# Feed-forward seven slots behind its attention up to batch 4, and a shorter list of loads behind each w1

## The chip, the cores and the metric

The kernel runs on one core of one Trainium2 chip. The time is device microseconds of that core for one execution. An execution is called fast here when it is not in the chip's slower state. A profile is one execution taken by the hardware profiler; its span (from the first instruction to the last) is 1.6 to 2.0 us shorter than the time of the same execution. In the views PE is TensorE, DVE is VectorE, ACT is ScalarE, POOL is GpSimd and SP is SyncE. L251 is the line of the `kx` and `qx` copies, L267 that of all transposes, L504 the gate's maximum and L511 the first of w1's three requests.

## The reference

Eight batches go through masked attention, and then each through a feed-forward of one expert, which a gate picks from the mean of the attention's output. Cut to what matters:

```python
# q, k, v: (8 batches, 8 heads, 576, 64) float32
scores = q @ k.T / 8           # heads 0-3: 0 <= rel < 32; heads 4-7: rel < 128 and rel % 4 == 0
x = softmax(masked scores) @ v # -> (8, 576, 512)

pooled = x.mean(axis=1)        # one expert for a whole batch
e = argmax(pooled @ w_gate)    # 8 experts
h = maximum(x @ w1[e], 0.0)    # w1[e]: 512 x 1024
out = gate_w * (h @ w2[e])     # w2[e]: 1024 x 512
```

For this argument it matters that w1 and w2 of a batch (2.1 MB each in float32) can't be requested before that batch's attention is done and its gate has been decided, and that every batch brings new q, k, v and new weights.

## The kernel before

All work is laid out by hand in **slots**. A batch's attention takes four slots (4b to 4b+3), the first two with heads 4 to 7 ("g = 1"), the others with heads 0 to 3 ("g = 0"). Its feed-forward is cut into 21 **pieces**: 16 of the first matrix product, four output blocks of the second, and a tail. `PIECES` says how many pieces each slot gets beside its attention; the count runs on from batch to batch.

```python
NSLOT = 4
PIECES = [0] * 7 + [6, 6, 5, 2, 2] + [8, 8, 2, 3] * 7   # slots 0 to 39
GO = (1, 0)                                             # order of the halves
```

So batch 0's feed-forward is spread over slots 7 to 11, and that of batch b from 1 on fills slots 4b+8 to 4b+11, eight slots after its attention began. The slots loop, with cuts:

```python
for t in range(7, len(PIECES)):
    cur, pre = sl[t], sl[t - 1]
    ...
    gb, gn = divmod(t - 5, NSLOT)
    if gn == 0 and 0 < gb < B:
        emit_gate(gb)                  # first thing in slot 4b+5
    ...
    run_T(t)                           # transposes of the k or q of slot t+2 or t+1
    pre.av_a(); ...; cur.s(); cur.x()  # attention
    ...
    for f in items[:k0]: f()           # feed-forward pieces
    pre.norm()                         # the last one of a batch also makes `pooled`
    for b, g, nm in tsched.get(t + 1, []):
        if g == 0:
            emit_pair(b, nm)           # VectorE copies kx, qx for the next slot's transposes
    for f in items[k0:]: f()
```

The gate, with the loads that it requests behind its w1. All these loads are issued by GpSimd, in this order, and land in this order:

```python
def emit_gate(b):
    ...
    nc.tensor.matmul(lg, lhsT=pooled..., rhs=wg_t...)    # 4 matmuls
    nc.vector.max_with_indices(mx[:], mi[:], lg)
    e_val = nc.values_load(mi..., engines=[ET.Pool], ...)  # GpSimd waits for the index
    nc.gpsimd.dma_start(out=w1b[:, 2:4, :], in_=moe_w1[ds(e_val, 1), 256:512, :]...)
    ...                                                   # and the other half of w1
    if b == 0:
        load_va(2); load_qb(2); load_w2(e_val, w2b); load_qa(3); load_vb(2)
    else:
        load_vb(b + 2)
        load_w2(e_val, w2b)
        load_qa(b + 3)     # k and q of heads 4-7
    load_va(b + 3)
    load_qb(b + 3)         # k and q of heads 0-3

def emit_pair(b, nm):      # heads 0-3 only
    x = ldp.tile([P, RH, 2, DH], BF16, name=f"{nm}x", ...)
    nc.vector.tensor_copy(out=x..., in_=loads[b][nm, 0][:])
```

The q, k and v requested behind the gate of batch b are those of batch b+3, a whole batch ahead of need (all but `load_vb`, which is for batch b+2). Outputs are stored by SyncE, one slot after they are made (1.18 MB per batch).

The softmax here doesn't subtract the row's maximum and nothing guards it: scores larger than these inputs give would overflow.

Of the kernel before, what the change touches and what calls it, by code (L numbers as in the profile page):

```python
# [20 lines left out]
B = 8  # L21
# [21 lines left out]
HALF = 288  # L43
NSLOT = 4
EARLY = 7

PIECES = [0] * 7 + [6, 6, 5, 2, 2] + [8, 8, 2, 3] * 7


@with_exitstack  # L50
def kernel(
# [42 lines left out]
    def bank():  # L94
        return psM.tile([P, 512], F32, name="m", tag="M", space=PSUM)[:]
# [12 lines left out]
    def load_tiles(b):  # L108
        t = {}
        for g in range(2):  # L110
            for nm in ("k", "q"):
                shape = [P, RJ, DH] if g else [P, 2, RH, DH]
                t[nm, g] = ldp.tile(shape, BF16, name=f"{nm}m{g}", tag=f"{nm}m{g}")
            t["v", g] = ldp.tile([P, 4, 4, DH], BF16, name=f"vm{g}", tag=f"vm{g}")
        t["vt", 0] = ldp.tile([KB, 4, DH], BF16, name="vt0", tag="vt0")
        t["vt", 1] = ldp.tile([KB, 4, 2, DH], BF16, name="vt1", tag="vt1")
        loads[b] = t

    def load_1(b, g, nm):
        i = src[nm][b, 4 * g : 4 * g + 4]  # L120
        if g == 0:
            i = bass.AP(tensor=i.tensor, offset=i.offset, ap=[[RH * DH, P], [2 * S * DH, 2], [1, RH * DH]])
            nc.gpsimd.dma_start(out=loads[b][nm, g][:].rearrange("p h j d -> p h (j d)"), in_=i)
        else:
            i = i.rearrange("h s d -> (h s) d").rearrange("(p j) d -> p j d", j=RJ)
            nc.gpsimd.dma_start(out=loads[b][nm, g][:], in_=i)

    def load_qk(b, g):
        for nm in ("k", "q"):
            load_1(b, g, nm)  # L130

    def load_v(b, g):
        t = loads[b]["v", g]
        if g == 0:
            for h in range(4):
                nc.gpsimd.dma_start(out=t[:, h], in_=v[b, h, 0:512, :].rearrange("(c p) d -> p c d", p=P))  # L136
        else:
            nc.gpsimd.dma_start(out=t[:], in_=v[b, 4:8, 0:512, :].rearrange("h (p j) d -> p h j d", j=4))

    def load_vt(b, g):  # L140

        vt = loads[b]["vt", g]
        if g == 0:
            nc.gpsimd.dma_start(out=vt[:], in_=v[b, 0:4, 512:S, :].rearrange("h p d -> p h d"))
        else:
            nc.gpsimd.dma_start(out=vt[:], in_=v[b, 4:8, 448:S, :].rearrange("h (p t) d -> p h t d", t=2))

    GO = (1, 0)

    def load_qa(b):  # L150
        if b < B:
            load_tiles(b)
            load_qk(b, GO[0])

    def load_va(b):
        if b < B:
            load_v(b, GO[0])
            load_vt(b, GO[0])

    def load_qb(b):  # L160
        if b < B:
            load_qk(b, GO[1])

    def load_vb(b):
        if b < B:
            load_v(b, GO[1])
            load_vt(b, GO[1])
# [75 lines left out]
    def half(a):  # L243
        return slice(64 * a, 64 * a + 64)
# [250 lines left out]
    def emit_gate(b):  # L495
        s = st[b]
        pooled = s["pooled"]
        lg = bank()[0:1, 0:E]
        for c in range(4):
            nc.tensor.matmul(lg, lhsT=pooled[:, c : c + 1], rhs=wg_t[:, c, :], start=(c == 0), stop=(c == 3))  # L500
        l_sb = small.tile([1, E], F32, name="l_sb", tag="l_sb")
        mx = small.tile([1, 8], F32, name="mx", tag="mx")
        mi = small.tile([1, 8], U32, name="mi", tag="mi")
        nc.vector.max_with_indices(mx[:], mi[:], lg)  # L504
        nc.vector.tensor_copy(out=l_sb[:], in_=lg)
        s["gate"] = (l_sb, mx)
        e_val = nc.values_load(mi[0:1, 0:1].bitcast(I32), engines=[ET.Pool], min_val=0, max_val=E - 1)
        w2b = wp.tile([P, 8, DM], BF16, name="w2b", tag="w2b")
        w1b = wp.tile([P, 4, F], BF16, name="w1b", tag="w1b")
        s["w1"], s["w2"] = w1b, w2b  # L510
        nc.gpsimd.dma_start(  # L511
            out=w1b[:, 2:4, :],
            in_=moe_w1[ds(e_val, 1), 256:512, :].rearrange("e (c p) f -> p (e c) f", p=P),
        )
        for a in range(2):
            nc.gpsimd.dma_start(
                out=w1b[half(a), 0:2, :],
                in_=moe_w1[ds(e_val, 1), 128 * a : 128 * a + 128, :].rearrange("e (h d) f -> d (e h) f", d=DH),
            )
        if b == 0:  # L520
            load_va(2)
            load_qb(2)
            load_w2(e_val, w2b)
            load_qa(3)
            load_vb(2)
        else:
            load_vb(b + 2)
            load_w2(e_val, w2b)
            load_qa(b + 3)
        load_va(b + 3)  # L530
        load_qb(b + 3)

    def load_w2(e_val, w2b):

        nc.gpsimd.dma_start(
            out=w2b[:].rearrange("p (x j) f -> p x (j f)", x=2),
            in_=moe_w2[ds(e_val, 1)].rearrange("e (x p j) f -> p (e x) (j f)", x=2, p=P),
        )
# [16 lines left out]
    def emit_gate_bc(b):  # L555

        gw = st[b]["gw"]
        gbc = small.tile([P, 1], F32, name="gbc", tag="gbc")
        nc.sync.dma_start(out=gbc[:], in_=gw[0:1, 0:1].to_broadcast([1, P]))
        st[b]["gbc"] = gbc  # L560


    def ffn1(b, fc, hf, eng, cs=(2, 3, 0, 1)):
        s = st[b]
        if fc == 0 and hf == 0 and "ht" not in s:
            s["ht"] = htp.tile([P, 8, S], BF16, name="ht", tag="ht")
        cols = slice(HALF * hf, HALF * hf + HALF)
        if 2 in cs:
            s["hm"] = bank()[:, 0:HALF]
        hm = s["hm"]  # L570
        for c in cs:
            w = s["w1"][:, c, F // 2 * (fc // 4) : F // 2 * (fc // 4) + F // 2].rearrange("p (m j) -> p j m", j=4)
            nc.tensor.matmul(hm, lhsT=w[:, fc % 4, :], rhs=s["xt"][:, c, cols], start=(c == 2), stop=(c == 1))  # L573
        if 1 not in cs:
            return
        o = s["ht"][:, fc, cols]
        if eng == "A":
            nc.scalar.activation(out=o, in_=hm, func=AF.Relu)  # L578
        else:
            nc.vector.tensor_scalar_max(out=o, in0=hm, scalar1=0.0)  # L580
# [3 lines left out]
    def flush():  # L584
        for f in stores:
            f()
        stores.clear()
# [40 lines left out]
    for b in range(B):  # L628
        for n in (0, 2):
            t = NSLOT * b + n  # L630
# [3 lines left out]
    def run_T(t):  # L634
        for b, g, nm in tsched.get(t, []):
            for f in emit_T(b, g, nm):
                f()
# [41 lines left out]

    sl = [slot(t) for t in range(len(PIECES))]  # L680

# [10 lines left out]
    nd_banks = {"0dk": (0, 1), "0pk": (0, 1), "1dk": (2, 1), "1dq": (0, 2)}  # L692
    evac = {}

    def piece(b, x, e):
        if x < 16:
            ffn1(b, x // 2, x % 2, e)
        elif x < 20:
            ffn2(b, x - 16, "AD"[x % 2])
        else:  # L700
            ffn_tail(b)
# [35 lines left out]
    done = 0  # L737
    for t in range(7, len(PIECES)):
        cur, pre = sl[t], sl[t - 1]
        n = PIECES[t]  # L740

        lead = t > 7 and n >= 5 and done % 21 < 16 and pre.on
        items = []
        for i, x in enumerate(range(done, done + n)):
            e = "A" if ((lead or t == 7) and i == 0) or 2 * i >= n else "D"
            items.append(lambda x=x, e=e: piece(x // 21, x % 21, e))
        done += n
        gb, gn = divmod(t - 5, NSLOT)
        if gn == 0 and 0 < gb < B:
            emit_gate(gb)  # L750
        if t == 7:
            items.pop(0)
            n -= 1
            dve, act = emit_T(2, GO[0], "q")
            dve()
            act()
        else:
            run_T(t)
            pre.av_a()
            flush()  # L760
            if (t == 8) if gb == 0 else gn == 2 and gb < B:
                emit_gate_bc(gb)
            cur.s()
            cur.x()
            if pre.on and not cur.on:
                items.pop(0)()
                n -= 1
            pre.av_b()
            if lead:
                items.pop(0)()  # L770
                n -= 1
            pre.ln()
            cur.mask()
            pre.rd()
        k0 = n // 2
        for f in items[:k0]:
            f()
        if t > 7:
            pre.norm()
        for b, g, nm in tsched.get(t + 1, []):  # L780
            if g == 0:
                emit_pair(b, nm)
        for f in items[k0:]:
            f()
        if (t == 7) if gb == 0 else gn == 1 and gb < B:
            emit_gate_w(gb)
# [31 lines left out]
```

## Time and profile before

| | before |
|---|---|
| time, median of the 3 runs that the prediction had (lowest to highest) | 211.54 us (211.29 to 211.74) |
| span of the profiled run | 210.9 us |
| PE busy | 192.6 us, 91% |
| loads' packets, share of 16 engines' span | 96.2% |
| distance of gates from 43 to 158 us (first matmul of a gate to that of the next) | 22.3 to 23.5 us |

PE's row is not to be read alone: PE and DMA are both nearly full until all of q, k and v are in. The prediction below shows those rows, and the waits that tell which of the two is ahead. One view: the busy time of each engine in the stretch from 57 to 150 us, which is the steady state (columns: stretch, its length; busy us and instructions of PE, PE's weight loads, VectorE, ScalarE, GpSimd; granted clock; mean share of DMA packets in flight; GB/s). Before:

```profile
57.00:150.00 93.00, 88.60 (x1444) 65.89 (x1452) 62.74 (x172) 66.79 (x136) 40.50 (x60) 1.00 1.25 222
```

PE works 88.6 of 93 us, at full clock. Beside this row stands a number of mine, worked out from the same DMA records: for each 0.1 us, how many packets of loads and stores were in flight, on 16 engines. What is missing to 16, as a share of 16 and summed up from 57 to 150 us, is called **DMA idle** below. It is 0.04 us before.

### The profile page before, as it was taken

The page shows a single profiled execution, that of the slowest core. Times are in us where ns is not written, and L with a number is a line of the kernel's source. Part 1 is how long each engine was busy: PE and PEld are TensorE (multiplying, and loading weights), DVE is VectorE, ACT ScalarE, POOL GpSimd, SP SyncE. Part 2 cuts the span into 40 slices and gives each one's busy share as a digit, 9 for nine tenths or more (in the row PEclk, how much of TensorE's full clock was granted, in tenths as well). Part 3 has the DMA queues.
Part 4 walks back from the last instruction along what each step waited for, and adds up shares of the span by engine and source line. Part 5 has one row for each costly group of instructions (what it writes and reads, how often), then busy time and mean ns, then how long its engine had stood idle before and what let it go on. Part 6 is the DMA issues. An engine that isn't in the chain of part 4 may idle for free.

```text
span 210.9 us, 6979 instructions
## 1 busy us (share of the span) xinstructions
PE 192.6 (91%) x2906; PEld 140.1 (66%) x2921; DVE 129.6 (61%) x359; ACT 135.0 (64%) x270; POOL 82.4 (39%) x130
## 2 busy tenths in 40 slices
PE   6866979989969999999999998989999999999991
PEld 1645757975658755895598656876589558749741
DVE  5476868676767657766777466765777465325312
ACT  2497796976648766886678864876698656332320
POOL 7977385239236262626362253626104000500000
PEclk9996557999999999999999999999999999999998
DMA  5999999999999999999999999999999994499223
GB/s 70 184 182 197 171 172 199 216 185 168 209 228 235 207 210 230 221 243 208 221 215 246 208 211 222 236 228 209 235 204 203 215 217 139 75 215 231 106 113 111
DMA packets 46415, 41.11 MB, mean 195 GB/s; under 512 B 24880, under 2 KB 34096, under 8 KB 46384
## 3 DMA queue, kind: packets, MB, share of 16 engines
q0 software_dynamic: 38784, 31.20, 96.2%
q1 hardware_dynamic: 7600, 9.46, 13.9%
q8 instruction: 23, 0.38, 0.7%
q14 instruction: 8, 0.07, 0.1%
HBM read 62.41 MB, written 9.44 MB: 341 GB/s over the span
## 4 chain that ended last, share of the span: by engine, by line
PE 58%; DMA 30%; issue 4%; ACT 2%; DVE 2%; POOL 1%; POOLq 1%; SPq 0%
PE m L573 21%; PE m L593 20%; DMA w1b<-in_moe_w_dram 15%; DMA qm<-in_q_dram 9%; DMA km<-in_k_dram 6%; PE n L353 5%; PE m L267 4%; PE m L608 3%; PE ps L288 2%; PE n L267 1%; PE m L500 1%; ACT pt L321 1%; ACT rd L468 1%; PE m L353 1%; DVE pt L328 1%
## 5 line engine op out<-in xcount | busy, mean ns | idle before, releaser
L573 PE MATMUL m<-xt,w1b 128*128 128x288 bf16 x512 | 67.2, 288 | 2.1 <-DMA w1b<-in_moe_w_dram 1.6
L573 PEld LDWEIGHTS <-w1b 128*128 128x128 bf16 x512 | 56.5, 114 | 8.1 <-issue 3.2
L593 PE MATMUL m<-w2b,ht 128*128 128x512 bf16 x241 | 56.9, 379 | 0.9 <-issue 0.2
L578 ACT ACTIVATE ht<-m 128x288 bf16<-128x288 f32 x77 | 31.6, 411 | 21.3 <-PE m L573 17.6
L593 PEld LDWEIGHTS <-ht 128*128 128x128 bf16 x256 | 24.1, 98 | 27.3
L484 DVE SCALAR_TENSOR_TENSOR xt<-n,rd 128x512 bf16<-128x512 f32 (+3 forms) x58 | 29.4, 545 | 10.1 <-ACT rd L468 10.1
L328 DVE TENSOR_TENSOR pt<-pt,mk 128x896 bf16<-128x896 bf16 x32 | 20.0, 625 | 21.7 <-ACT pt L321 21.7
L275 ACT ACTIVATE qk<-m 128x512 bf16<-128x512 bf16 (+1 forms) x27 | 19.9, 739 | 16.9 <-PE m L267 16.8
L321 ACT ACTIVATE pt<-ps 128x896 bf16<-128x896 f32 x32 | 29.0, 905 | 2.8 <-PE ps L288 2.8
L136 POOL DMA_DIRECT2D vm<-in_v_dram x32 | 24.0, 763 | 10.8 <-DMA qm<-in_q_dram 4.3
L272 DVE COPY qk<-m 128x640 bf16<-128x640 bf16 (+1 forms) x29 | 23.0, 797 | 6.7 <-PE m L267 6.6
L580 DVE TENSOR_SCALAR ht<-m 128x288 bf16<-128x288 f32 x51 | 22.8, 456 | 6.4 <-PE m L573 5.4
L600 DVE TENSOR_SCALAR osb<-m,gbc 128x512 f32<-128x512 f32 x16 | 12.0, 750 | 17.6 <-PE m L593 17.6
L468 ACT ACTIVATE rd<-lnd 128x576 f32<-128x576 f32 x32 | 21.9, 684 | 1.0
L353 PE MATMUL n<-pt,ones 64*64 64x64 bf16 (+6 forms) x262 | 21.2, 250 | 1.2 <-DVE pt L328 1.0
L463 ACT ACTIVATE lnd<-n 128x512 f32<-128x512 f32 (+3 forms) x58 | 20.6, 406 | 0.9 <-PE n L353 0.9
L511 POOL DMA_DIRECT2D w1b<-in_moe_w_dram x8 | 5.7, 716 | 38.3 <-DVE ht L580 18.0
L353 PE MATMUL n<-pt,vm 64*64 64x96 bf16 (+3 forms) x606 | 20.4, 203 | 0.2
L353 PEld LDWEIGHTS <-vm 64*64 64x64 bf16 x672 | 15.7, 112 | 3.3 <-SPq L421 1.5
L598 ACT ACTIVATE osb<-m,gbc 128x512 f32<-128x512 f32 x16 | 10.9, 682 | 8.7 <-PE m L593 8.7
L353 PEld LDWEIGHTS <-ones 64*64 64x64 bf16 x288 | 12.7, 112 | 5.3 <-issue 1.9
L288 PE MATMUL ps<-qk 64*64 64x96 bf16 (+3 forms) x608 | 14.9, 210 | 1.3 <-ACT pt L321 1.1
(72 smaller groups left out, 199.7 us busy)
## 6 DMA issues: line engine op xcount, KB each, us to landing
w2b<-in_moe_w_dram POOLq DMA_DIRECT2D x8, 1024.0 KB, 11.5
out_dram<-osb SPq DMA_DIRECT2D x32, 256.0 KB, 6.9
km<-in_k_dram POOLq DMA_DIRECT2D x16, 288.0 KB, 11.6
qm<-in_q_dram POOLq DMA_DIRECT2D x16, 288.0 KB, 11.5
w1b<-in_moe_w_dram POOLq DMA_DIRECT2D x8, 512.0 KB, 11.5
w1b<-in_moe_w_dram POOLq DMA_DIRECT2D x16, 256.0 KB, 11.0
vm<-in_v_dram POOLq DMA_DIRECT2D x8, 256.0 KB, 9.6
vm<-in_v_dram POOLq DMA_DIRECT2D x32, 64.0 KB, 10.1
```

The lines of the kernel that those rows point to most:

```text
L136: nc.gpsimd.dma_start(out=t[:, h], in_=v[b, h, 0:512, :].rearrange("(c p) d -> p c d", p=P))
L272: nc.vector.tensor_copy(out=ev[x][0], in_=ev[x][1])
L321: nc.scalar.activation(out=pt[:], in_=s["ps"][:, :, 0:NP], func=AF.Exp, scale=0.125)
L328: nc.vector.tensor_tensor(out=pt[:], in0=pt[:], in1=mk[:, g : g + 1, :].to_broadcast([P, 2, NP]), op=ALU.mult)
L353: x = nc.tensor.matmul(oo, lhsT=lhsT, rhs=rhs, start=start, stop=True, skip_group_check=True)
L463: nc.scalar.activation(out=lnd[:, lo : lo + w], in_=ndc(o, w), func=AF.Ln)
L468: nc.scalar.activation(out=rd[:], in_=s["lnd", n][:], func=AF.Exp, scale=-1.0)
L484: nc.vector.scalar_tensor_tensor(out=o, in0=i0, scalar=1.0, in1=i1, op0=ALU.mult, op1=ALU.mult, accum_out=s["pool"][:, w, c : c + 1])
L573: nc.tensor.matmul(hm, lhsT=w[:, fc % 4, :], rhs=s["xt"][:, c, cols], start=(c == 2), stop=(c == 1))
L578: nc.scalar.activation(out=o, in_=hm, func=AF.Relu)
L580: nc.vector.tensor_scalar_max(out=o, in0=hm, scalar1=0.0)
L593: nc.tensor.matmul(om, lhsT=s["ht"][:, fc, r * P : (r + 1) * P], rhs=s["w2"][:, fc, :], start=(fc == 0), stop=(fc == 7))
```

## The change

The intent: the feed-forward starts one slot earlier (seven slots behind its attention) for batches 1 to 5, the thin stretch of 21 pieces in five slots moves from batch 0 to batch 5, and w1 no longer stands behind loads that nobody needs yet, since only what the slots up to the next gate read is requested behind it. The diff, with cuts at `...`:

```diff
-PIECES = [0] * 7 + [6, 6, 5, 2, 2] + [8, 8, 2, 3] * 7
+PIECES = [0] * 7 + [8, 8, 2, 3] * 5 + [6, 6, 4, 3, 2] + [8, 8, 2, 3] * 2
...
-        if b == 0:
-            load_va(2)
-            load_qb(2)
-            load_w2(e_val, w2b)
-            load_qa(3)
-            load_vb(2)
-        else:
+        if 0 < b < B - 2:
+            load_1(b + 2, GO[0], "q")
+        if b < B - 2:
+            load_1(b + 2, GO[1], "k")
+        load_w2(e_val, w2b)
+        if b < B - 2:
+            load_va(b + 2)
+            load_1(b + 2, GO[1], "q")
             load_vb(b + 2)
-            load_w2(e_val, w2b)
-            load_qa(b + 3)
-        load_va(b + 3)
-        load_qb(b + 3)
+        if b < B - 3:
+            load_tiles(b + 3)
+            load_1(b + 3, GO[0], "k")
...
-            items.append(lambda x=x, e=e: piece(x // 21, x % 21, e))
+            if x % 21 == 0 and t > 7:
+                items.append(... (piece(x // 21, 0, e, (2, 3)), piece(x // 21, 1, e, (2, 3)), piece(x // 21, 0, e, (0, 1))))
+            elif x % 21 == 1 and t > 7:
+                items.append(... piece(x // 21, 1, e, (0, 1)))
+            else:
+                items.append(... piece(x // 21, x % 21, e))
...
-        if gn == 0 and 0 < gb < B:
-            emit_gate(gb)
...
-        for f in items[k0:]:
+        for i, f in enumerate(items[k0:]):
+            if i == len(items) - k0 - 1 and t % NSLOT == 0 and t // NSLOT - 1 < B:
+                emit_gate(t // NSLOT - 1)
             f()
```

"Second q" below is the q of heads 0 to 3 (`GO[1]`), which goes through the VectorE copy `qx`; "first q" and "first k" are those of heads 4 to 7. The other edits let the first two pieces start on the half of w1 that lands first, and put the gate ahead of the last piece of slot 4b+4, instead of at the start of slot 4b+5.

More of the change, by code (lines that the diff above doesn't have):

```diff
@@ L568, in ffn1 @@
         if 2 in cs:
-            s["hm"] = bank()[:, 0:HALF]
-        hm = s["hm"]
+            s["hm", fc, hf] = bank()[:, 0:HALF]
+        hm = s["hm", fc, hf]
         for c in cs:
@@ L693, with piece @@
     evac = {}
-    def piece(b, x, e):
+    def piece(b, x, e, cs=(2, 3, 0, 1)):
         if x < 16:
-            ffn1(b, x // 2, x % 2, e)
+            ffn1(b, x // 2, x % 2, e, cs)
         elif x < 20:
@@ L745 @@
             e = "A" if ((lead or t == 7) and i == 0) or 2 * i >= n else "D"
-            items.append(lambda x=x, e=e: piece(x // 21, x % 21, e))
+            if x % 21 == 0 and t > 7:
+                items.append(lambda x=x, e=e: (piece(x // 21, 0, e, (2, 3)), piece(x // 21, 1, e, (2, 3)), piece(x // 21, 0, e, (0, 1))))
+            elif x % 21 == 1 and t > 7:
+                items.append(lambda x=x, e=e: piece(x // 21, 1, e, (0, 1)))
+            else:
+                items.append(lambda x=x, e=e: piece(x // 21, x % 21, e))
         done += n
         gb, gn = divmod(t - 5, NSLOT)
-        if gn == 0 and 0 < gb < B:
-            emit_gate(gb)
         if t == 7:
```

## The prediction

> **What bounds the kernel now.** I read the page first, then PE's waits, then the chain of waits, then the issue and landing time of every DMA.
>
> ```profile
> span 210.9 us, 6979 instructions
> ...
> PE   6866979989969999999999998989999999999991
> ...
> DMA  5999999999999999999999999999999994499223
> ...
> q0 software_dynamic: 38784, 31.20, 96.2%
> ```
>
> PE looks like the bound: 192.6 of 210.9 us busy. But the DMA row is full from the second slice (5 us) to slice 33, and thins out only when q, k and v are all in. Two resources are nearly full at once, so the question is who waits for whom. PE's timeline at two places, one batch apart:
>
> ```profile
> 117.13 0.56 PE L267 MATMUL m<-identb,km 128*128 128x128 bf16 x7 [0.20 <-DMA km<-in_k_dram]
> 141.19 0.51 PE L267 MATMUL m<-identb,km 128*128 128x128 bf16 x6 [0.80 <-DMA km<-in_k_dram]
> ```
>
> The first transpose of each batch waits for its k. The k loads of batches 4 to 7 land at 72.05, 94.37, 117.09 and 141.14 us, and their transposes start at 72.10, 94.44, 117.13 and 141.19: always 0.04 to 0.07 us later. So this load sets the pace, at (141.14-72.05)/3 = 23.0 us per batch. PE alone needs 22.33 us per batch (83.14 to 105.47, one batch without a stall). The chain of waits agrees:
>
> ```profile
> 115.31 13.27 DMA w1b<-in_moe_w_dram
> 128.58 0.29 issue
> 128.87 12.27 DMA km<-in_k_dram
> 141.14 0.05 issue
> 141.19 0.68 PE m L267 x9
> ```
>
> A 288 KB load takes 12 us because it stands behind others: at most 8 GpSimd requests are out (each waits for the eighth before it to land), and they land in order. The same kind of request on an empty queue, against a full one (all DMAs issued from 112 to 113.5 us, then from 159.5 to 161.5):
>
> ```profile
> w1b<-in_moe_w_dram POOLq DMA_DIRECT2D x1, 512.0 KB, 14.1
> ```
>
> ```profile
> w1b<-in_moe_w_dram POOLq DMA_DIRECT2D x1, 512.0 KB, 5.2
> ```
>
> The difference is queue, but a queue that never runs dry is also what keeps the DMA engines working. Verdict: from 60 to 141 us the kernel is DMA-bound by a hair (23.0 against 22.3), afterwards PE-bound (174 to 207 us: 32.45 of 33 busy).
>
> **What the Trainium skill says.** "DMA: Bandwidth & Descriptors", section "Anatomy of one DMA", puts a fixed cost of about 2 us on a DMA beside bytes over 436 GB/s. The trace agrees roughly: the 512 KB w1 request (1.05 MB in HBM as float32) lands after 5.2 us on an empty queue, while half of a 1024 KB w2 takes about 2.7 in a full queue (38.26 to 43.69 us for the whole one of batch 0), so 2.5 us are latency that only a queue hides. The same page, "Issuing engines are not separate DMA queues", says that DMAs from all engines share the 16 DMA engines; so the output stores slow the loads. The trace agrees (0.74 us per 256 KB store, below). "TensorE: Matmul & The Clock Gate", "Architectural detail", calls VectorE strict FIFO, which makes the gate's maximum wait for whatever stands before it; the trace has them in program order.
>
> **The change part by part.** No work is added or removed: same bytes, matmuls and evictions. Three things move.
>
> (1) Feed-forward of batches 0 to 5 starts one slot earlier, and the thin stretch (21 pieces in five slots) moves from batch 0 to batch 5. When slot 27 starts, the kernel before has 3 pieces of batch 4 left: two output blocks of 1.8 us and a tail of 1.0, 4.6 us of PE. That is the most it can bring, if slot 27 starts no later. The kernel before starts it at 146.2 us, so break-even is 150.8.
>
> (2) The gate comes before the last piece of slot 4b+4, half a microsecond earlier, but w1 is now needed two slots later instead of three.
>
> (3) The prefetch behind w1 shrinks by about a batch. Per group the new order is w1, q, k, w2, v, q, v, k. The second q is needed for a copy on VectorE (`qx`) in slot 4b+8, which stands before the maximum of the next gate:
>
> ```profile
> 110.44 0.58 DVE L251 COPY qx<-qm 128x1152 bf16<-128x1152 bf16 x1
> 111.36 0.16 DVE L504 MAX8 mx<-m 1x8 f32<-1x8 f32 x1 [0.34 <-PE m L500]
> ```
>
> ```profile
> 113.12 0.72 POOL L511 DMA_DIRECT2D w1b<-in_moe_w_dram  x1 [2.38 <-PE n L353]
> ```
>
> From the start of the maximum to the issue of w1 is 1.76 us; the copy before it takes 0.5. So the next w1 can't be requested until the second q has landed, plus 2.3 us. Before, that q had been requested a batch earlier.
>
> Cost of one group: differences of consecutive landings from 30 to 156 us, fitted by least squares with the store bytes in the same interval (86 loads, rms 0.28 us): w1 3.29+2x1.28 = 5.85; w2 5.17; four q/k 2x1.43+2x1.47 = 5.80; v of one half 1.24+0.30, of the other 4x0.39+0.30; sum 20.2. Stores 0.74 per 256 KB, 4.5 of them per batch: 3.3. Together 23.5, against 23.0 seen from k to k.
>
> The loop after the change: after the second q come one half's v (1.86) and a k (1.47), 3.3 us of service. The next w1 is issued 2.3 us after that q, with about 1.0 us still to land, and has 2.5 us of latency: the DMA engines idle for about 1.5 us at each gate. Period: 23.0 to 23.5 plus 1.5 = **24.5 to 25 us**, against 23.0 before.
>
> Walk: slot 7 does two pieces more (1 us), slot 8 starts at about 39, gate 1's matmuls at 44.2, w1 is issued at about 45.8; its q lands 8 (w1) + 1.4 + 0.7 (store) later, 56 us, just as PE comes to slot 11. Four periods of 24.75 on, slot 27 starts at 56.3+99 = 155.3, instead of 150.8 for break-even: 4.5 us lost. A check without the loop: a DMA that never idles would deliver k of batch 7 at 141.1 as now, then w1 of batch 5 (5.85) and the q for slot 27 (1.4): 148.4 at the earliest; five gates at 1.5 us of idle make 155.9.
>
> In slots 27 and 28 (thin now) PE needs 9.3 us, but the second q of batch 7 lands k 1.4 + w2 5.2 + v 1.5 + q 1.4 + stores 1.7 = 11.3 us after the first, and its copy takes 0.5: a wait of about 2.4 us. Then PE alone, as before. Sum: 211.5+4.5+2.4 = 218.4 us.
>
> **Rivals.** (a) The author's hope: w1 no longer queues, PE's stalls between 34 and 146 us go (0.34+0.54+0.98+0.98+0.44+0.20+0.59+0.80 = 4.9 us), and the 4.6 us of filler use them. For it: PE idles 0.98 at slot 12 for w1 in the kernel before. Against: DMA can't deliver before 148.4, so the best end is 211.5-(150.8-148.4) = 209.1, that is -1.1%; over 2% faster needs loads that run faster than any in the trace. (b) Stores fall elsewhere and the idle at the gate is only 0.5 us: slot 27 at 151, then the thin slots' wait: 211 to 214. (c) PE's gaps halve the clock again, as from 17.7 to 34.8 us, where PE was 64% busy at full clock just before: 5 us more. Against: the new waits are 1 to 2.5 us between dense matmuls, and 1 us gaps near 58 and 61 left the clock at 1.00. (d) The output blocks wait for w2 in their slots: w2 lands about 3 us before them, so no.
>
> **Range and chances.** The mechanism gives 216 to 220. I know the queue's idle per gate to half a microsecond at best, five times over (2.5), and stores' timing to as much. A change so finely set may rest on something I miss, so I shade towards rival (b): **217.5 us**, range 210.5 to 223. Faster by over 2% (under 207.3) 0.07; within 2% 0.22; slower (over 215.8) 0.71.
>
> **What will show it.** Right: PE waits of about 1.3 us before the transposes of `qm` (slots 15, 19, 23, 27) and of `qx`, one each per batch, and none for w1; `qx` on VectorE waiting for the q load, just before each gate; the DMA row with a dip at each gate; gates 24.5 to 25 us apart; the first w1 request landing in about 5.5 us instead of 10 to 14; slot 27's transpose at about 155. Wrong: gates 22.3 to 23 apart, `qx` not waiting, or loads of a group that take under 20 us with the stores. Then the end falls to 209 or below 212. A halved clock after 40 us would make it worse than the range.

## The result, and the profile after

| | before | after |
|---|---|---|
| time, median of 4 (lowest to highest) | 211.55 us (211.29 to 211.74) | 231.54 us (230.26 to 232.46) |
| span of the profiled run | 210.9 us | 229.1 us |
| gates' distances, from the second gate on | 22.6, 22.9, 22.3, 23.5, 23.3 | 23.3, 25.8, 26.1, 26.3, 29.0 |
| start of slot 27 | 146.2 us | 164.0 us |
| from there to PE's last matmul | 60.3 us | 60.8 us |
| DMA idle, 57 to 150 us | 0.04 us | 4.60 us |
| bytes of loads landed in that stretch (as bf16) | 15.95 MB | 14.08 MB |

The changed kernel is slower: ratio 1.094, with an interval from 1.088 to 1.100. Ratios are the mean time of one kernel's fast runs over that of the other kernel's fast runs of the same rounds, so they are not quite the ratio of the medians quoted here. All four runs lie above the predicted range (210.5 to 223).

The page of the profile after, the lines that answer to the four of before in the prediction:

```profile
span 229.1 us, 6992 instructions
...
PE   5577989999996989699996999799398899999992
...
DMA  5999999969999999989999999979999896199423
...
q0 software_dynamic: 38784, 31.20, 90.5%
```

The DMA row, which had no digit under 9 from slice 2 to slice 33, now has dips at slices 9, 18 and 27, just after the gates at 44.7, 93.8 and 146.2 us: there the queue has run dry. (The gates at 68.1 and 120.0 don't show in this row, since the share of a slice can exceed 1; the DMA idle counts them.) PE has dips of its own in slices 13, 17, 22, 26 and 29, one per batch. What happens at a gate, on VectorE (columns: start, busy time, engine, line, operation; in brackets the idle time before it and what ended it):

```profile
96.18 0.46 DVE L251 COPY qx<-qm 128x1152 bf16<-128x1152 bf16 x1 [2.48 <-DMA qm<-in_q_dram]
96.56 0.15 DVE L504 MAX8 mx<-m 1x8 f32<-1x8 f32 x1
```

The same two instructions as in the prediction, one batch of the changed kernel: the copy `qx` now waits 2.48 us for its q load, which lands at 96.16, and the gate's maximum stands behind it. PE and GpSimd at the same gate:

```profile
96.70 0.77 PE L267 MATMUL m<-identb,qx 128*128 128x128 bf16 x7 [1.89 <-DVE qx L251]
```

```profile
98.28 0.70 POOL L511 DMA_DIRECT2D w1b<-in_moe_w_dram  x1 [2.72 <-PE n L353]
```

PE has nothing to do for 1.89 us, and w1 is issued at 98.28, 2.12 us after that q landed. In the other gates it is 2.06 to 2.12 us as well: q lands at 70.28, 122.13 and 148.19, w1 goes out at 72.34, 124.25 and 150.31. How long requests now take from issue to landing, that w1 and the next second q:

```profile
w1b<-in_moe_w_dram POOLq DMA_DIRECT2D x1, 512.0 KB, 5.1
```

```profile
qm<-in_q_dram POOLq DMA_DIRECT2D x1, 288.0 KB, 18.2
```

The w1 got what the change was to give it: 5.1 us instead of 14.1. The second q pays, 18.2 us, because the whole group stands before it. And since the next w1 needs that q, the groups form a ring. The chain of waits after is that ring (start, us, what):

```profile
52.34 17.95 DMA qm<-in_q_dram
...
78.12 18.03 DMA qm<-in_q_dram
...
103.95 18.18 DMA qm<-in_q_dram
...
130.02 18.17 DMA qm<-in_q_dram
```

Four times the request for a second q, 25.8, 25.8 and 26.1 us apart: these are the laps of the ring. The waits of PE, and those of VectorE for `qx` (us in total, times, longest):

```profile
PE m L267 <- DVE qx L251: 7.7, 5, 1.9
PE m L267 <- DMA qm<-in_q_dram: 5.4, 3, 3.9
```

```profile
DVE qx L251 <- DMA qm<-in_q_dram: 9.5, 5, 2.5
```

No wait for w1 is left in PE's list, where it stood first after the warm-up before. The steady state in the view of before:

```profile
57.00:150.00 93.00, 84.14 (x1329) 61.96 (x1329) 56.53 (x159) 61.29 (x125) 32.97 (x49) 0.96 1.19 203
```

In the same 93 us PE is busy for 84.14 us instead of 88.60 and does 1329 matmuls in the trace instead of 1444 (some records can be missing, so the counts are good to a few per cent), and the clock is no longer 1.00: it is halved from 97.0 to 100.4, 124.3 to 127.7 and later 165.3 to 168.7 us. The last of the three:

```profile
165.30:168.70 3.40, 3.40 (x28) 2.22 (x21) 1.20 (x3) 2.41 (x6) 0.74 (x1) 0.50 1.13 207
```

### The profile page after: what moved, and what is told of

It reads as the page before. It is cut to its first block, busy times and chain, and to the rows that moved or that the text cites. A ratio compares the mean times of both kernels' runs of the same rounds, so it can differ in the third digit from the quotient of the medians.

```text
span 229.1 us, 6992 instructions
## 1 busy us (share of the span) xinstructions
PE 199.8 (87%) x2921; PEld 142.1 (62%) x2921; DVE 130.1 (57%) x359; ACT 136.2 (59%) x270; POOL 82.4 (36%) x130
## 4 chain that ended last, share of the span: by engine, by line
DMA 40%; PE 32%; POOL 7%; DVE 7%; issue 6%; ACT 5%; POOLq 1%; SPq 0%
DMA qm<-in_q_dram 37%; PE m L574 12%; PE m L594 11%; PE n L353 4%; DMA vm<-in_v_dram 3%; PE m L267 3%; DVE xt L484 2%; ACT qk L275 2%; POOL w1b L516 2%; POOL km L123 1%; ACT rd L468 1%; ACT pt L321 1%; DVE pt L328 1%; POOL vm L138 1%; POOL w2b L536 1%
## 5 line engine op out<-in xcount | busy, mean ns | idle before, releaser
L574 PE MATMUL m<-xt,w1b 128*128 128x288 bf16 x512 | 69.9, 292 | 0.5 <-ACT qk L275 0.3
L594 PE MATMUL m<-w2b,ht 128*128 128x512 bf16 x256 | 60.0, 390 | 0.0
L594 PEld LDWEIGHTS <-ht 128*128 128x128 bf16 x256 | 24.6, 100 | 29.5 <-issue 3.0
L484 DVE SCALAR_TENSOR_TENSOR xt<-n,rd 128x512 bf16<-128x512 f32 (+3 forms) x58 | 29.3, 543 | 11.9 <-ACT rd L468 11.7
L275 ACT ACTIVATE qk<-m 128x512 bf16<-128x512 bf16 (+1 forms) x27 | 20.1, 743 | 23.5 <-PE m L267 23.1
L136 POOL DMA_DIRECT2D vm<-in_v_dram x32 | 23.9, 756 | 22.7 <-DMA km<-in_k_dram 7.2
L581 DVE TENSOR_SCALAR ht<-m 128x288 bf16<-128x288 f32 x51 | 21.9, 454 | 6.9 <-PE m L574 6.4
L353 PE MATMUL n<-pt,ones 64*64 64x64 bf16 (+6 forms) x262 | 22.5, 261 | 1.0 <-DVE pt L328 0.8
L353 PE MATMUL n<-pt,vm 64*64 64x96 bf16 (+3 forms) x606 | 21.1, 209 | 1.6 <-DVE xt L484 1.3
L353 PEld LDWEIGHTS <-vm 64*64 64x64 bf16 x672 | 16.7, 118 | 5.4 <-SPq L421 1.8
L144 POOL DMA_DIRECT2D vt<-in_v_dram x8 | 5.0, 628 | 33.8 <-DMA w2b<-in_moe_w_dram 33.2
L288 PE MATMUL ps<-qk 64*64 64x96 bf16 (+3 forms) x608 | 15.6, 214 | 1.4 <-ACT pt L321 0.8
```

The costliest lines, as they stand in the source:

```text
L136: nc.gpsimd.dma_start(out=t[:, h], in_=v[b, h, 0:512, :].rearrange("(c p) d -> p c d", p=P))
L275: nc.scalar.activation(out=ev[x][0], in_=ev[x][1], func=AF.Copy)
L353: x = nc.tensor.matmul(oo, lhsT=lhsT, rhs=rhs, start=start, stop=True, skip_group_check=True)
L484: nc.vector.scalar_tensor_tensor(out=o, in0=i0, scalar=1.0, in1=i1, op0=ALU.mult, op1=ALU.mult, accum_out=s["pool"][:, w, c : c + 1])
L574: nc.tensor.matmul(hm, lhsT=w[:, fc % 4, :], rhs=s["xt"][:, c, cols], start=(c == 2), stop=(c == 1))
L581: nc.vector.tensor_scalar_max(out=o, in0=hm, scalar1=0.0)
```

## The experiments

The theory that I set out to test, **A**: the second q is the last thing needed before a gate, the gate is needed before the next w1, and so the group's whole service plus an empty queue becomes the period. Rivals: **B**, the new places of the feed-forward cost the time, not the loads; **C**, the loads themselves are served more slowly in the new order, so that mending the links of the ring leaves most of the loss. The halved clock is a suspect of its own (e7). Before's medians in the three sets of rounds were 212.56, 212.28 and 212.00 us; each ratio is to the runs of its own rounds.

| run | median us | ratio to before (95%) | DMA idle 57-150, us |
|---|---|---|---|
| after | 231.54 | 1.094 (1.088 to 1.100) | 4.60 |
| e1 schedule only | 217.54 | 1.022 (1.016 to 1.028) | 0.37 |
| e2 requests only | 224.13 | 1.056 (1.049 to 1.064) | 3.19 |
| e3 gate before copy | 228.45 | 1.073 (1.067 to 1.080) | 1.75 |
| e4 no stores in the loop | 213.41, one run, state unknown | | 10.42 |
| e5 first q, second k a gate earlier | 223.99 | 1.056 (1.050 to 1.061) | 0.39 |
| e6 second q ahead of w2 | 224.18 | 1.061 (1.055 to 1.067) | 2.70 |
| e7 keep PE busy | 229.78 | 1.084 (1.080 to 1.089) | 5.12 |
| e8 before, k first | 212.37 | 1.003 (0.999 to 1.006) | |
| e9 e1 without thin slots | 216.56 | 1.024 (1.018 to 1.030) | |
| e10 before, gate early | 213.01 | 1.005 (1.001 to 1.008) | |
| e11 before, no stores | 210.12, one run, state unknown | | 3.2 |
| e12 e5 and e6 together | 223.03 | 1.053 (1.049 to 1.058) | 0.63 |

### The two halves of the change

**e1, the new schedule with the old list of loads** (lines of the list joined here).

```diff
-        if 0 < b < B - 2:
-            load_1(b + 2, GO[0], "q")
-        ... (the rest of the new list)
+        if b == 0:
+            load_va(2); load_qb(2); load_w2(e_val, w2b); load_qa(3); load_vb(2)
+        else:
+            load_vb(b + 2); load_w2(e_val, w2b); load_qa(b + 3)
+        load_va(b + 3); load_qb(b + 3)
```

> The changed kernel with the request order of the kernel before: seven slots' lag, early gate and split first pieces alone. Theory A (the shallow request list, not the lag, makes the loss: each gate waits for the second q, and the DMA queue runs dry): the queue stays full, the first k of each batch again lands about 23 to 24 us after the last one, gates 23 to 24 us apart, but w1 of batch 5 now has to be there for slot 27 and stands behind k and q of batch 7 (152.7 us before), so 213 to 218 us. Theory B (two slots between gate and w1 are too few, whatever the list): w1 stands 13 us in the queue and PE waits 3 to 5 us for it in every batch, gates 26 us apart again, 226 us or more.

It took 217.54 us (216.93 to 218.66), 2.2% over before, with an interval that holds 2%. Gates are 22.9, 22.8, 22.6 and 23.0 us apart after one of 26.4. The steady state and PE's waits:

```profile
57.00:150.00 93.00, 90.32 (x1444) 66.05 (x1441) 62.08 (x169) 67.15 (x136) 40.53 (x60) 0.98 1.24 222
```

```profile
PE m L574 <- DMA w1b<-in_moe_w_dram: 2.8, 3, 2.1
...
PE n L353 <- DVE xt L484: 1.3, 2, 1.0
PE m L500 <- DVE pooled L492: 0.9, 1, 0.9
PE m L267 <- DVE kx L251: 0.9, 1, 0.9
```

With the old list there is no ring: 222 GB/s and 1444 matmuls, as before. So the greater part of the loss is not in the schedule, against B. But the schedule alone costs some 5 us, and where is worth seeing. Slot 27 starts at 152.0 us, 5.8 later than before, with 4.6 us of feed-forward more done. All of these 5.8 us are there by the gate of batch 2 (71.8 against 65.7): the first slots hold more pieces, PE waits 2.1 us for the w1 of batch 1, and the clock is halved from 61.5 to 64.9. (The profiled run was the slowest of e1's four.) If that work were handed back in the slots that follow, the end would be 1.2 us later. It isn't: from there to PE's last matmul it takes 60.5 us, before 60.3. The thin slots 27 to 31 have too little feed-forward to lie beside attention's own chain, and PE waits there for w1 (0.36), `kx` (0.87), `pooled` (0.94) and `xt` (0.98 and, just behind, 0.31), 3.5 us together. The thin stretch took back what it was to bring.

**e2, the old schedule with the new list.** The edit to the kernel before is the second hunk of the change's diff alone, from `if b == 0:` to `load_1(b + 3, GO[0], "k")`.

> The kernel before with the request order of the changed one; lag, gate and pieces as before. Theory A: the same loop (second q, its copy on VectorE, gate, w1, ... second q) sets the period, so gates 25.5 to 26.5 us apart, qx waits for its load, and 228 to 236 us. Theory B (the lag is to blame): w1 has three slots again, gates 22.5 to 23.5 us apart, 210 to 215 us.

It took 224.13 us (223.02 to 225.54), ratio 1.056. PE's two longest waits:

```profile
PE m L267 <- DVE qx L251: 8.8, 7, 2.8
PE m L267 <- DMA qm<-in_q_dram: 3.9, 5, 1.9
```

The new list makes the waits of the ring with the old schedule too, with gates 24.0, 25.0, 26.7, 23.5 and 24.4 us apart. A is right in kind, though the time is 4 us under what I expected of it; B is out. Schedule and list add 2.2% and 5.6%, their sum is 7.8%, and together they make 9.4%.

### Inside the ring

**e3, the gate ahead of the `qx` copy.** In slot 4b+4 the copy is emitted behind the gate, so that the maximum need not wait for the second q.

```diff
-        for b, g, nm in tsched.get(t + 1, []):
-            if g == 0:
-                emit_pair(b, nm)
+        ... (pairs() is the loop taken out above)
+        late = t % NSLOT == 0 and 0 < t // NSLOT - 1 < B
+        if not late:
+            pairs()
         for i, f in enumerate(items[k0:]):
             if i == len(items) - k0 - 1 and ...:
                 emit_gate(t // NSLOT - 1)
+                if late:
+                    pairs()
```

> The changed kernel with one edit: VectorE's copy of the second q is put after the gate's maximum instead of ahead of it. Same bytes, same request order. Theory A: w1 is asked for 2.1 us after the gate's matmuls although the second q is still under way, the queue doesn't run dry, gates 24 to 24.7 us apart instead of 26, 221 to 226 us. Theory C (the loss is DMA work and depth alone, the copy's place doesn't matter): gates still 25.8 to 26.3 apart, 229 to 232 us.

It took 228.45 us (227.45 to 230.08), ratio 1.073. DMA idle falls from 4.60 to 1.75 us, as A says, but the gates are still about 25 us apart on average, and PE still waits for `qx` (8.5 us in seven waits). So the link from q to w1 was real, but cutting it gives 2 points of the 9: PE waits for the same q anyway, since its transposes come right behind. The result lies between what A and C expected, and both missed.

**e4, no stores of batches 0 to 4 (the result is wrong).**

```diff
-        stores.append(lambda: nc.sync.dma_start(out=out[b, r * P : ...], in_=osb[:]))
+        if b > 4:
+            stores.append(lambda: nc.sync.dma_start(out=out[b, r * P : ...], in_=osb[:]))
...
-        for a in range(2):
+        for a in range(2 if b > 4 else 0):
```

> Wrong result on purpose: the changed kernel without the output stores of batches 0 to 4; everything else as it is. It measures the term of the period that stores make up. Fit over the changed kernel's loads: 0.86 us per 256 KB, 3.9 us per batch. Theory A: the loop from one w1 request to the next shrinks from 26 to 22.3-23 us, 213 to 218 us. If stores cost only what the prediction had (3.3) or less: 23 to 24 us apart, 218 to 223 us. Theory D (the loop is latency, stores are hidden): 25.5 to 26 apart, 228 us or more.

It took 213.41 us in its one run (state unknown), inside what A expected. The steady state:

```profile
57.00:150.00 93.00, 92.08 (x1516) 68.39 (x1514) 63.78 (x176) 69.19 (x141) 41.65 (x62) 1.00 1.13 174
```

PE is busy for 92.08 of 93 us, and the gates are 22.4 to 23.1 us apart: without the stores the ring is shorter than PE's own work. This run also measures a term of the prediction. From the landing of w1 to the landing of the second q the group took 11.7, 11.5 and 11.3 us (77.2 to 88.9, 100.5 to 112.0, 123.3 to 134.6); in the changed kernel it took 15.7, 16.0 and 16.0 (80.50 to 96.16, 106.12 to 122.13, 132.23 to 148.19). The difference, **4.4 us per batch**, is what 1.18 MB of stores cost the loads there: all of a batch's stores fall into this stretch, and the queue never runs dry in it, with the stores or without. The prediction had 3.3; a fit like its own over the changed kernel gave 3.9 (0.86 per 256 KB), and e11 measures the old order below.

**e5, the first q and the second k requested one gate earlier**, so that only w2, v and the second q stand behind w1.

```diff
-        if 0 < b < B - 2:
-            load_1(b + 2, GO[0], "q")
-        if b < B - 2:
+        if b == 0:
             load_1(b + 2, GO[1], "k")
...
             load_1(b + 3, GO[0], "k")
+            load_1(b + 3, GO[0], "q")
+            load_1(b + 3, GO[1], "k")
```

> The changed kernel with two requests moved across the gate: the first q of a batch and its second k are asked for at the end of the group before, not right behind w1. Same lag, same bytes; 6.2 us of loads now stand behind the second q instead of 3.3, so the queue still holds about 4 us of work when w1 is asked for. Theory A (an empty queue at each gate): DMA idle under 1 us between 57 and 150 us (4.6 in the changed kernel), gates 23 to 24.3 us apart, 216 to 222 us, near the 217.5 of the schedule alone. Theory C (this order of loads and stores is slower in itself, depth doesn't matter): gates 25.5 us or more apart, 228 us or more.

It took 223.99 us (222.38 to 224.52), ratio 1.056. The queue no longer runs dry (DMA idle 0.39 us), and the gates are 22.6, 23.1, 23.9, 26.3, 23.3 and 24.7 us apart. Slot 27 starts at 153.3, close to where e1 has it. The time is 2 us over what A expected: two stretches of halved clock (118.7 to 122.2 and 166.5 to 173.4) and a `qx` wait of 2.28 us came behind it. The steady state shows what is still missing against e1:

```profile
57.00:150.00 93.00, 88.52 (x1420) 64.73 (x1426) 60.17 (x167) 65.91 (x134) 38.25 (x57) 0.98 1.24 210
```

The share of packets in flight is that of e1 (1.24), but the rate is 210 against 222 GB/s. The queue doesn't run dry, and still less comes through: this is C's part.

**e6, the second q ahead of w2.**

```diff
             load_1(b + 2, GO[1], "k")
+            load_1(b + 2, GO[1], "q")
         load_w2(e_val, w2b)
         if b < B - 2:
             load_va(b + 2)
-            load_1(b + 2, GO[1], "q")
             load_vb(b + 2)
```

> The changed kernel with the second q asked for ahead of w2 instead of behind w2 and v. Depth over the gate in bytes is as in the changed kernel, but the q that the gate's maximum stands behind lands 6 to 7 us earlier. Theory A: the gate no longer waits for a load, w1 is asked for with about 2 us of queue left, no qx waits, gates 23.5 to 24.7 us apart, 219 to 225 us. Theory C: gates 25.5 or more apart, 228 us or more.

It took 224.18 us (223.03 to 226.34), ratio 1.061, inside what A expected. After 40 us no wait for `qx` is left. The transposes of the first q now wait 6.6 us in six waits, and attention waits 2.3 us for v. The order within a group only decides who waits for the group.

**e7, PE kept busy while it waits:** eight dummy matmuls ahead of the transposes where the waits fall.

```diff
         else:
+            if t % NSLOT == 1 and 9 < t < 30:
+                busy(8, bank())
             run_T(t)
```

> The changed kernel with eight dummy matmuls of 512 columns (1.7 us at full clock) ahead of the transposes of qx in slots 13, 17, 21, 25 and 29, where PE waits for the load. They fill the wait. Theory A (the period is a loop of DMA and VectorE): the clock drops of 3.4 us after 97, 124 and 165 us get fewer, but gates stay 25.7 to 26.3 us apart, and the time falls by 0 to 2 us: 229.5 to 232. Theory F (PE's gaps halve the clock, and that is the extra loss over the prediction): 224 to 227 us.

It took 229.78 us (229.25 to 230.45), ratio 1.084, and only one stretch of halved clock is left from 40 us up to the last batch's matmuls, 175.7 to 179.1. The gates are 25.9, 25.9, 26.4, 24.2 and 25.1 us apart. So the halved clock is worth about one point of the nine. It is a consequence of the waits and not the main cause of the loss.

**e12, e5 and e6 together:** the first q and the second k a gate earlier, and the second q ahead of w2.

```diff
-        if 0 < b < B - 2:
-            load_1(b + 2, GO[0], "q")
-        if b < B - 2:
+        if b == 0:
             load_1(b + 2, GO[1], "k")
+        if b < B - 2:
+            load_1(b + 2, GO[1], "q")
         load_w2(e_val, w2b)
...
-            load_1(b + 2, GO[1], "q")
...
             load_1(b + 3, GO[0], "k")
+            load_1(b + 3, GO[0], "q")
+            load_1(b + 3, GO[1], "k")
```

> The changed kernel with both edits that each gained about 7 us: first q and second k asked for one gate earlier (e5), second q asked for ahead of w2 (e6). Theory A (what is left in e5 is the wait for q of batch 7 in the thin slots, 2.3 us, and the halved clock after it, 166 to 173 us; what is left in e6 is an empty queue at the gate): neither is left, it comes near the schedule alone, 216.5 to 219.5 us. Theory C (the two edits mend the same thing): 222 to 224.

It took 223.03 us (222.20 to 223.88), ratio 1.053, what C expected and not A. After 40 us no wait for q is left, the queue doesn't run dry (0.63 us), and now it is again w1 that PE waits for:

```profile
PE m L575 <- DMA w1b<-in_moe_w_dram: 6.1, 4, 3.0
```

Its w1 lands 7.2 to 8.6 us after its issue and is needed two slots after its gate. The two edits mend the same thing, so their gains don't add. Between 57 and 150 us e12 lands 14.65 MB of loads with 0.63 us of idle; e1 lands 15.68 MB with 0.37. That shortfall of 7% is not in the idle time, and no run of mine tells its cause. The DMA records tell where it lies: in this stretch the packets of w1 (2048 bytes) took 203 ns in e12 and 173 ns in the kernel before, those of the first k and q (2304 bytes) 224 and 192 ns, while those of w2 (4096 bytes) took 323 and 332, and those of 128 bytes 32 in both.

### Other ways to the same end

**e9, e1 without the thin slots.**

```diff
-PIECES = [0] * 7 + [8, 8, 2, 3] * 5 + [6, 6, 4, 3, 2] + [8, 8, 2, 3] * 2
+PIECES = [0] * 7 + [8, 8, 2, 3] * 8
```

> The schedule-alone kernel (217.5 us) without its thin stretch: seven slots' lag for all batches, 39 slots instead of 40. Same pieces and requests. In the schedule-alone kernel slots 27 to 31 held 4.6 us less of feed-forward than the kernel before and yet took 26.7 us against 27.3: PE waited 3.5 us there for attention's own chain (0.36 w1, 0.87 kx, 0.94 pooled, 0.98 and 0.31 xt). Theory A (thin slots give their PE time back as waits): the waits go, 3 to 4 us faster, 213.5 to 215. Theory G (it is w1 and the loads of batch 7 that hold slots 27 to 31): no gain, 217 or more.

It took 216.56 us (215.51 to 218.40), ratio 1.024 against e1's 1.022: nothing gained. The waits of the thin slots are gone, and one for w1 took their place:

```profile
PE m L574 <- DMA w1b<-in_moe_w_dram: 4.6, 4, 2.5
```

The wait of 2.5 us is for the w1 of batch 7, whose feed-forward now comes two slots behind its gate with no attention left beside it. I had expected a gain of some 3 us. The thin stretch is not the cause of a loss that could be dropped: something has to fill the two slots between a gate and its w1 at the end as well.

**e8, the kernel before with the first k ahead of v and w2**, to take away its waits for k.

```diff
         else:
+            if b + 3 < B:
+                load_tiles(b + 3)
+                load_1(b + 3, GO[0], "k")
             load_vb(b + 2)
             load_w2(e_val, w2b)
-            load_qa(b + 3)
+            if b + 3 < B:
+                load_1(b + 3, GO[0], "q")
```

> The kernel before with one edit: the k of batch b+3, whose landing set its pace, is asked for right behind w1, ahead of v and w2 (which are needed 1.6 us later or more). Queue depth and bytes unchanged. If the kernel before is held by that k as read from its trace: its waits (0.2 and 0.8 us) go, others take over part of it since DMA stays full: 0.5 to 1.5 us faster, 210 to 211 us. If its PE is the bound: no change within 0.3 us.

It took 212.37 us (211.28 to 213.29), ratio 1.003, the same. The k waits did vanish from the profile (k now lands at 63.2, 85.1, 108.0 and 131.5 us, some 9 us earlier, and the profiled span was 209.5 us, that of the fastest of its six runs), but the six timed runs show none of it: before's own runs beside them go from 210.99 to 213.63, and a gain under half a per cent can't be seen in that. I had expected 0.5 to 1.5 us. The waits for w1 did not get shorter: 1.7 us in all, of which 1.5 are one wait, against 1.6 before.

**e10, the kernel before with the early gate and the split first pieces** only, that is the change's diff with the old `PIECES` and the old list of loads:

```diff
-        if gn == 0 and 0 < gb < B:
-            emit_gate(gb)
...
-        for f in items[k0:]:
+        for i, f in enumerate(items[k0:]):
+            if i == len(items) - k0 - 1 and t % NSLOT == 0 and t // NSLOT - 1 < B:
+                emit_gate(t // NSLOT - 1)
             f()
```

> The kernel before with only the early gate and the split first pieces of the change; lag of eight slots and its own request order. w1 is asked for 0.5 us earlier, and a missing second half of w1 can hide behind 0.5 us of the first half's matmuls. Its w1 waits of 1.57 us could shrink to about 0.7: 210.7 to 211.5 us, within 0.5% of the kernel before. If the queue alone fixes when w1 lands, no difference.

It took 213.01 us (211.99 to 213.80), ratio 1.005, the same, where I had expected it to be up to 0.9 us faster or unchanged. The waits for w1 are gone, but the gate's matmuls now wait for `pooled`, six times, 2.4 us in all.

**e11, the kernel before without the stores of batches 0 to 4 (wrong).** The edit is that of e4, in the kernel before.

> Wrong result on purpose: the kernel before without the output stores of batches 0 to 4. If the kernel before is DMA-bound by a hair between 60 and 141 us, as the prediction says, then with 3 us of DMA work less per batch PE becomes the bound: k lands well ahead of its transposes, PE's waits after 60 us (2.7 us in the profile) go, gates 22.3 us apart, 207.5 to 209.5 us. If stores cost nothing there, 211 to 212.5.

It took 210.12 us in its one run (state unknown), 0.9% under before and a little over what I had expected. Gates are 22.3 us apart, PE's own pace, and k lands at 88.6, 108.0 and 130.4 us, 5.5 to 8.4 us ahead of its transposes, the first of which start here without a wait:

```profile
94.12 0.67 PE L267 MATMUL m<-identb,km 128*128 128x128 bf16 x9
```

So the kernel before is bound by its transfers, but only by a hair, as predicted; and with no stores in the loop at all there is about 1% to win, as far as one run can tell. The same pair of runs gives the price of the stores in the old order: from one first k to the next the loads took 22.3 and 22.7 us in the kernel before (72.05 to 94.37 to 117.09) and 19.9 and 19.4 here (68.69 to 88.61 to 108.01), with a queue that didn't run dry in either. The same stores cost 2.4 and 3.3 us there, against 4.4 in the new order.

No variant with a right result beats the kernel before. Of the 9.4%, the schedule alone makes 2.2 (e1). With the links of the ring mended, 5.3 to 6.1 are left (e12, e5, e6), so the links make 3 to 4. What lies between, another 3 to 4 points, is C's: loads that are served more slowly, for a reason that stays open. The parts need not add up exactly.

## Why the prediction was wrong

The direction and the mechanism were right, the size was not: 217.5 us against 231.5. In the profile the loss is 18.2 us; the walk in the prediction gave 6.9. Step by step:

**What bounds the kernel before: right.** e11 takes the stores away, k lands 5.5 to 8.4 us ahead of its transposes, and the gates come at 22.3 us. e8 shows the other side: with an earlier k alone nothing can be measured, so k was the load that PE happened to wait for, and not a limit by itself.

**The ring: right.** The second q is landed, copied, and w1 is issued 2.06 to 2.12 us later (predicted 2.3). w1 lands in 5.1 to 5.3 us at the gates of batches 1 to 4 (predicted 5.5). The waits for w1 are gone. Those for `qx` came at four gates (1.5 to 1.9 us), those for `qm` only in slots 11, 15 and 27 and not in each batch. DMA idle is 4.6 us, nearly all of it at the three gates that the stretch holds in full, 1.3, 1.5 and 1.6 us (predicted 1.5). e2 has this ring with the old schedule, and e1 has none of it with the new one.

**The period: mis-sized, and here the step "Stores 0.74 per 256 KB, 4.5 of them per batch: 3.3" failed.** e4 measures 4.4 us, 1.1 more. With it the predicted period of 24.75 becomes 25.85; measured are 25.8, 26.1 and 26.3. The 0.74 came from a fit over the kernel before, where the same bytes are stored beside other loads, and there it was about right (e11: 2.4 and 3.3 us per batch). Why a store costs the loads more in the new order is open. Three periods at that size are 3.9 us of the miss, and slot 11 came 1.1 us later than the walk had it (57.4 against 56.3). The fourth period was 28.4 us, 3.6 more than predicted, since the first request of batch 5's w1 took 7.6 us and not 5.2. Its cause is open. It isn't bound to this place: in e7 that request took 5.2 us, but batch 4's took 6.7. Nor would all of the 3.6 us have been won without it: in e7 slot 27 starts at 159.3, yet PE's last matmul ends only 1.2 us earlier than in the changed kernel (223.5 against 224.8), as PE then waits for the second q behind it. Together slot 27 starts at 164.0 and not at 155.3.

**The credit of 4.6 us for feed-forward already done: wrong.** This is the step "That is the most it can bring, if slot 27 starts no later ... break-even is 150.8". The text calls it the most it can bring, but the walk then takes it in full. e1 shows that it brings nothing: 60.5 us from slot 27 to PE's end, against 60.3 before. In the thin slots PE waited 3.5 us for w1, `kx`, `pooled` and `xt`; I read this as attention's own chain through ScalarE and VectorE, which has become longer than PE's work, so that what PE no longer had to do, it waited. In the changed kernel it is 60.8 us where the prediction had 58.1 (its 2.4 us wait for `qx` included, which didn't come: the second q landed 11.4 us after the first, as predicted, at 175.34, but PE needed 12.1 us for slots 27 and 28, and not 9.3). That is 2.7 us of the miss; the halved clock of 165.3 to 168.7 us, 1.7 us of work lost, is within it. With 3.9, 1.1 and 3.6 this makes 11.3, the whole of 18.2 less 6.9.

**Rival (c), a halved clock: dismissed, and partly true.** "1 us gaps near 58 and 61 left the clock at 1.00" was the ground for it. The gaps that came were 1.5 to 3.9 us, and behind three of them the clock was halved for 3.41 us each, up to 5.1 us of PE's work. Most of that seems to be hidden in the wait for the next q: e7, which has only one such stretch, is just one point faster.

**Rivals (a) and (b) did not come:** slot 27 at 164 is past both.

One slip of the text has no weight: batch 0's feed-forward does not start a slot earlier. It starts in slot 7 in both kernels and only ends earlier, which the walk has right ("slot 7 does two pieces more").

The timed medians differ by 20.0 us and the profiled spans by 18.2; the rest is the spread of runs (the profiled run of before took 212.69 us, 1.1 over its median, that of after 230.87, 0.7 under its own).

## What to carry to other kernels

When two resources are nearly full, a deep queue of loads that are not yet needed is what keeps one of them full; before cutting it to shorten one request's way, look for what the next request waits for, and whether that wait closes a ring with the last load of the group. A ring's period is the sum of everything in it, stores included, so measure the stores' share in that order (one run without them) instead of taking it from another order. Work moved out of a stretch is only worth what that stretch is bound by: where PE has little to do, it may just wait for the other engines, as it did here.

## What the Trainium skill lacked or had wrong

- "TensorE: Matmul & The Clock Gate" ("What's actually happening") lets the clock fall to half after at least one idle window of about 3.4 us, and the section "HAM oscillation" gives the rule of no PE-idle gaps above that. Here much less was enough. The halved stretches start a whole number of 3.413 us windows apart (97.00, 124.31 and 165.27 us: 8 and 12 windows), so the page's free-running window agrees. But in the changed kernel the windows ahead of them were idle for 59%, 51% and 61%, with gaps of 1.89 and 1.74 us in the first two. In the 14 traces here, from 40 to 205 us, each of the 13 halved stretches (in eight traces) followed a window in which PE was idle for 46 to 87%; of the windows idle for 43% or less none brought on a new one, and three at 49%, 50% and 53% did not either. A gap of 1.80 us ending at 70.83 did no harm: a window's border cut it in two, and the two windows were idle for 23% and 33%.
- "DMA: Bandwidth & Descriptors", "Issuing engines are not separate DMA queues", says that DMAs run on the same 16 engines whichever engine issues them, as loads and stores do here; no page says how much a store costs the loads beside it, or whether this depends on their order. Here 1.18 MB of stores cost 2.4 and 3.3 us in the old order (e11; 3.3 by the fit) and 4.4 us in the new one (e4).
- "DMA: Bandwidth & Descriptors", "Specifications", gives about 358 GB/s as a core's limit of HBM, in a row that doesn't say when it holds. In the kernel before w2's 2.10 MB took 5.43 us in a full queue (38.26 to 43.69), 386 GB/s, and 5.17 us by the prediction's fit, 406 GB/s. "Perfetto Trace Analysis", "Roofline", has the condition: the figure is a core's share when both cores of a pair load, and a core alone can pull more, up to about 435 GB/s.
- No page has the price of a short list of outstanding loads. Cut from a batch ahead to the next gate, the loads of 57 to 150 us fell by 12%, from 15.95 to 14.08 MB. The idle of 4.6 us explains 5 points of it; the other 7 (a shortfall also seen in e12, whose queue doesn't run dry) stay open.
